# Order of the first feed-forward visits, and ten warm-up matmuls, in a float32 H3 + FFN kernel

## The chip, the cores and the metric

The kernel runs on one core of a Trainium2 chip. The metric is the device time of one execution in microseconds (us); lower is better. Its engines work side by side, each with its own instruction stream: TensorE (PE in the profile, its weight loads PEld), VectorE (DVE), ScalarE (ACT), GpSimd (POOL) and SyncE (SP), which here only issues DMAs.

## The reference

```
xn  = layernorm(q)                                   # q: 2048 x 576
kv  = shift_conv(k, 4 taps) * v
y   = irfft(rfft(kv, 4096) * rfft(ssm_k, 4096))[:2048] + kv * ssm_D
out = q + xn * y + relu(xn @ w1) @ w2                # w1: 576 x 4608, w2: 4608 x 576
```

Everything is float32. `q` has two uses: it is the input of the layer norm and it is added to the result.

## The kernel before

**Numbers.** A product of float32 matrices is made of three products of rounded parts: high by high, high by low, low by high. So each operand is split: ScalarE makes the high part by a copy into the rounded type, VectorE (activations) or GpSimd (weights, `split_lo`) makes the low part by a subtraction.

**Feed forward.** The 16 row tiles (128 rows each) form four row blocks of four tiles. The 4608 hidden columns form 18 chunks of 256 (`n`, two parts `j` of 128). The kernel goes twice over the 18 chunks, with two row blocks each time. The list `visits` says in which order a chunk meets a row block; `s` is the slot (0 or 1) that holds a block's operands. Before the change the list begins (chunk 0, slot 0), (chunk 0, slot 1), (chunk 1, slot 1), (chunk 1, slot 0), (chunk 2, slot 0). In a visit of the first half `mm1` makes the hidden values, for each part j 14 matmuls of 512 columns (line 548) into one of two PSUM banks, and `relu` leaves a high part `hh` (ScalarE, line 530) and a low part `ll` (VectorE, line 531). The second product is cut into units: `phase` queues eight units (four row tiles, two halves of 288 output columns) for one or two chunks, and `fill` issues them between the parts of later visits: as many as make up two chunks' worth at a time. A unit has 6 matmuls for each chunk (line 611), gathers in one of three PSUM buffers, and VectorE adds it to `acc` (line 615 for the first row block, 619 for others). The second half of the feed forward uses another form of the first product (`quad`, line 524), which the change does not touch.

**The start.** Input tiles of the first block are loaded in two pairs by SP and ACT. `keep_warm` runs matmuls on a zero tile (line 1082). `first_xT` takes the first block's rows: centred on VectorE or ScalarE, transposed by TensorE (line 255) and split into the operands `b1`, `b2`, `xr`; `WARM_TILE` gives how many warm-up matmuls the code puts behind the transposes of each of the four tiles. The division by the standard deviation is left to line 615. The second block (`second_xT`) is treated otherwise: statistics (line 172), `inv_std`, then `normalized` (line 187), transposes (line 271), splits. It is issued in one piece after the first visit and one `fill`.

**Weights.** `load_w1` loads a chunk of w1 into one tile `r1` (a single buffer with ten slots of 256 columns, five of which are used in the first half), `load_w2` half a chunk of w2 (two buffers). `split_plain`, `split_rest` and `split_w2` split them; the results lie in pools `g` and `w2` of four buffers each. `at_turn` puts a split's ScalarE part behind the latest relu that was issued.

**Order.** The code's order is a priority. A scheduler that simulates the program fixes each engine's instruction stream ahead of the run: it may put an instruction that it holds ready ahead of an earlier one that waits. `tc.issue_after` puts the instructions of a block behind a given one of the same engine. On the chip each stream runs in order.

**Convolution.** `conv` is a generator with three stages: forward transforms of the kernel and of kv (line 664), the middle (line 883), the inverse (lines 1024 and 1025). `tick` advances it in step with the feed forward, whose work counts in columns; `START` is the amount of feed forward ahead of its first step, and enters the rate as well:

```python
clock = {"ffn": 0.0, "conv": 0.0, "until": START, "done": False}
rate = FFT_TOTAL / (SHARE * FFN_TOTAL - PAUSES * PAUSE - START)
```

Of the kernel before, what the change touches and what calls it, by code (L numbers as in the profile page):

```python
# [10 lines left out]
F32 = mybir.dt.float32  # L11
F32R = mybir.dt.float32r
# [5 lines left out]
P = 128  # L18
# [8 lines left out]
FT = 2  # L27
FC = FT * P
NPAIR = DFF // FC
# [10 lines left out]
GR = P // (2 * A2)  # L40
NG = A1 // GR
N_WARM = 21
WARM_TILE = (0, 4, 0, 2)


W_PLAIN = 2 * 14 * 512
W_STAGE = (12 * HR, 12 * HR, 12 * HR + 2 * 512, 6 * HR + 2 * 512)
W_UNIT = 12 * NH
PAUSE = 16000
START = 12000  # L50
SHARE = 0.97


# [56 lines left out]
def h3_ffn_kernel(ctx: ExitStack, tc, x, k, v, shift_k, ssm_k, ssm_D, w1, w2, fwd, inv, mid, out):  # L110
# [35 lines left out]

    acc = {}

    def halves(u):

        return slice(u * A1, (u + 1) * A1), slice((1 - u) * A1, (2 - u) * A1)
# [8 lines left out]
    def load_x(t, tag, bufs, **queues):  # L160
        pair = xp.tile([P, 2, D], F32, tag=tag, name=f"acc{t}", bufs=bufs)
        move(pair, x, slice(t, t + 2), **queues)
        return pair

    def load_acc(t, **queues):
        pairs[t] = load_x(t, f"acc{t // BT % HB}", BT // 2, **queues)
        acc[t], acc[t + 1] = pairs[t][:, 0, :], pairs[t][:, 1, :]

    def stats(t, src):
# [40 lines left out]
    def split_low(c, ps, s):  # L210

        if c == 4:
            xr = ops[s, "xr"]
            done["act"] = nc.scalar.activation(xr[:64, :], ps[:64, :], AF.Copy)
            done["dve"] = nc.vector.tensor_tensor(xr[64:, :], ps[:64, :], xr[:64, :],
                                                  OP.subtract)
            return None
        to = ops[s, "b2" if c % 2 else "b1"][:, :, c // 2]
        last = nc.scalar.activation(to[:, 0], ps, AF.Copy)  # L219
        nc.vector.tensor_tensor(to[:, 1], ps, to[:, 0], OP.subtract)  # L220
        return last

    def row_tiles(s, name):
        t = scratch(s, name)
        return [t[:, i * D:(i + 1) * D] for i in range(BT)]

    def plain_tiles(s):
        for name in ("b1", "b2", "xr"):
            operand(s, name)

    def first_xT(srcs):

        plain_tiles(0)
        ps = []
        for c in range(5):
            ps.append(ps_o.tile([P, 512], F32, tag="o", name=f"psx{c}") if c >= 3 else fft_psum())
        neg = xp.tile([P, BT], F32, tag="neg", name="neg", bufs=1)
        behind = None
        rows = row_tiles(0, "xn0")
        for t in range(BT):  # L240
            xn = rows[t]
            if t % 2 == 0:
                with tc.issue_after(behind.ins) if behind else nullcontext():
                    stats(t, srcs[t])
                    behind = centred(xn, srcs[t], t)
            else:
                nc.scalar.activation(xn, srcs[t], AF.Copy, scale=-1.0 / D,
                                     accum_out=neg[:, t:t + 1])
                done["act"] = nc.scalar.activation(xn, srcs[t], AF.Identity,
                                                   bias=neg[:, t:t + 1])  # L250
                with tc.issue_after(done["act"].ins):
                    (split_plain if t == 1 else split_rest)(0, 0)
            for c in range(5):
                w = min(P, D - c * P)
                nc.tensor.transpose(ps[c][:w, t * P:(t + 1) * P], xn[:, c * P:c * P + w], ident)
            keep_warm(WARM_TILE[t])
        for c in range(5):
            last = split_low(c, ps[c], 0)
            if c == 1:
                with tc.issue_after(last.ins):  # L260
                    split_plain(0, 1)
        with tc.issue_after(done["dve"].ins):
            for t in range(1, BT, 2):
                stats(t, srcs[t])
            inv_std(0, BT)

    def turned(c, xn):
        w = min(P, D - c * P)
        ps = fft_psum()
        for i in range(BT):  # L270
            nc.tensor.transpose(ps[:w, i * P:(i + 1) * P], xn[i][:, c * P:c * P + w], ident)  # L271
        return ps
# [5 lines left out]

    def second_xT(srcs):

        plain_tiles(1)
        with tc.issue_after(done["acc"].ins):
            for t in range(BT + 2, HT):
                stats(t, srcs[t])
            inv_std(BT, BT)
        xn = row_tiles(1, "xn1")
        for cols in (slice(0, P), slice(P, D)):
            for i, row in enumerate(xn):
                normalized(row, srcs[BT + i], BT + i, cols)
        for c in range(5):  # L290
            split_low(c, turned(c, xn), 1)

    def later_xT(b):

# [128 lines left out]

    def load_w1(n):
        f0 = (n % NPAIR) * FC
        r1 = wp.tile([P, 10, FC], F32, tag="r1", name=f"r1_{n}", bufs=1)
        for o, step in ((0, P), (P, FC - P)) if n == 0 else ((0, FC),):
            f, to = slice(f0 + o, f0 + o + step), slice(o, o + step)
            queue = nc.gpsimd if n == 0 and o == 0 else nc.sync
            queue.dma_start(r1[:, :4, to], w1[:4 * P, f].rearrange("(c p) f -> p c f", p=P))  # L430
            for h in range(2):
                queue.dma_start(r1[64 * h:64 * h + 64, 4, to], w1[4 * P:, f])
        raw_w[n] = r1
        weights[n] = {}

    def load_w2(n, h):
        f0 = (n % NPAIR) * FC
        r2 = wp.tile([P, FT, NH], F32, tag="r2", name=f"r2_{n}_{h}", bufs=2)
        nc.sync.dma_start(r2, w2[f0:f0 + FC, h * NH:(h + 1) * NH]
                          .rearrange("(j p) d -> p j d", p=P))  # L440
        raw_w[n, h] = r2

    def group(n, k):
        return wp.tile([P, 2, 4, P], F32R, tag="g", name=f"g{n}_{k}", bufs=4)

    def split_into(n, hi, lo, src):
# [14 lines left out]
    def split_rest(n, j=None):  # L461
        f = slice(0, FC) if j is None else slice(j * P, (j + 1) * P)
        hi, lo = (m[:, f] for m in rest_flat(n))
        split_into(n, hi, lo, raw_w[n][:, 4, f])
# [41 lines left out]
    def split_w2(n, h):  # L506
        r2 = raw_w[n, h]
        t = wp.tile([P, 2, FT, NH], F32R, tag="w2", name=f"w2_{n}_{h}", bufs=4)
        with at_turn(n):
            nc.scalar.activation(t[:, 0], r2, AF.Copy)  # L510
        last = split_lo(t[:, 1], r2, t[:, 0])
        weights[n]["w2", h] = t
        return last
# [556 lines left out]
    for t in range(0, BT, 2):  # L1070
        load_acc(t, queues=(nc.sync, nc.scalar))
    load_w1(0)
    for h in range(2):
        load_w2(0, h)
    table = const.tile([P, 1], F32, name="table")
    nc.vector.memset(table, 1.0)
    nc.scalar.activation(table, table, AF.Sqrt)
# [10 lines left out]
    first_xT(acc)  # L1088
    with tc.issue_after(done["act"].ins):
        split_rest(0, 1)  # L1090
    for t in range(BT, HT, 2):
        load_acc(t)
    load_w1(1)
    for h in range(2):
        with tc.issue_after(done["act"].ins):
            done["pool"] = split_w2(0, h)
        load_w2(1, h)
    visits = []
    for half in range(HALVES):
        for m in range(NPAIR):  # L1100
            visits += [(half * NPAIR + m, (m + half + v_) % 2) for v_ in range(2)]
    ahead = (step for b_ in range(HB, NB) for step in later_xT(b_))

    def split_next(n, second, st):
# [21 lines left out]
        elif n + 1 < HALVES * NPAIR:  # L1126
# [4 lines left out]
            else:  # L1131
                sum_w(n + 1, st)

    for q, (n, s) in enumerate(visits):
        half, m = divmod(n, NPAIR)
        b = half * HB + s
        second = q % 2
        if q == 1:
            fill()
            second_xT(acc)  # L1140
        parts = quad(n, s, q % 2) if half else None
        for st in range(4):
            if half:
                next(parts)
            elif st % 2 == 0:
                mm1(n, s, st // 2)
                if q == 0:
                    done["acc"] = lows[-1]
            if q == 0 and st == 2:
                second_stats(acc)  # L1150
            split_next(n, second, st)
            if st == 1 and n:
                split_w2(n, second)
                if n + 1 < HALVES * NPAIR:
                    load_w2(n + 1, second)
            if half:
                tick(W_STAGE[st])
            if q > 3 and (st % 2 or st == 2 and q % 2):
                next(ahead, None)
            fill()  # L1160
        if m == NPAIR - 1 and not half:
            fetch(s, ("b1", "b2", "xr"))
        if n == NPAIR - 2 and not half:
            for _ in ahead:
                pass
            fetch(s, ("t",))
        last = m == NPAIR - 1
        if second == 0:
            phase([n] if m == 0 else [n - 1, n], s, b, last)
        elif last:  # L1170
            phase([n], s, b, True)
        if half == 1 and m == 0:
            base = HT + (1 - second) * BT
            for t in range(base, base + BT, 2):
                load_acc(t)
# [30 lines left out]
```

## Time and profile before

| | |
|---|---|
| runs | 1070.07 us median of 3 (1069.26 to 1071.27) |
| profiled execution, span from first to last instruction | 1071.0 us |
| TensorE busy | 1054.1 us (98%), 7147 matmuls |
| VectorE busy | 748.2 us (70%) |
| ScalarE busy | 549.7 us (51%) |
| GpSimd busy | 397.5 us (37%) |
| mean granted TensorE clock | 0.994 |
| DMA, mean | 191 GB/s |

The page of the profile has no other figure for the profiled execution's own time than its span. A line of a timeline reads: start, duration (for a merged group from its first start), engine, line of the code, operation, output <- input, shape, count, and in brackets the idle time of the engine just before and what ended it. A line of stretches reads: stretch, its length, busy time and count of each engine, granted clock, DMA share, GB/s.

### The profile page before, as it was taken

To read this page: it belongs to the slowest core of one execution; us is meant where nothing else is said; L and a number is where in the kernel's file an instruction comes from. 1 tells how busy PE (TensorE), PEld (TensorE's weight loads), DVE (VectorE), ACT (ScalarE), POOL (GpSimd) and SP (SyncE) were. 2 spreads that over 40 slices of the span, in tenths; PEclk is the share of its full clock that TensorE was granted. 3 is DMA by queue.
4 is the path that set the end of the run, shared out by engine and by line. 5 is a ranking of instruction groups with operands and counts; after the bars stand their busy time and mean duration, and the time that the engine had idled before them with its cause. 6 is when DMAs were issued, how large, how long until landed. Compare 5 with 4: busy or idle time off the path is not lost.

```text
span 1071.0 us, 19976 instructions
## 1 busy us (share of the span) xinstructions
PE 1054.1 (98%) x7147; PEld 991.6 (93%) x7147; DVE 748.2 (70%) x1314; ACT 549.7 (51%) x1201; POOL 397.5 (37%) x398
## 2 busy tenths in 40 slices
PE   7999999999999999999999999999999999999998
PEld 5789999899999999999999999999999998999998
DVE  5437777789876788752487887778777773666764
ACT  4225556534433434332387777777777763444430
POOL 3133333333333332223334434433434444454541
PEclk9999999999999999999999999999999999999999
DMA  7674757687857666755985556655645549866844
GB/s 183 142 176 127 201 163 204 177 244 225 237 165 179 185 179 200 238 153 185 306 247 180 162 168 185 180 181 170 196 141 177 170 147 295 256 220 193 246 144 111
DMA packets 156303, 204.45 MB, mean 191 GB/s; under 512 B 32845, under 2 KB 122703, under 8 KB 155180
## 3 DMA queue, kind: packets, MB, share of 16 engines
q1 hardware_dynamic: 143308, 189.00, 59.6%
q0 software_dynamic: 12576, 13.44, 5.5%
q8 instruction: 56, 0.92, 0.4%
q10 hardware_dynamic: 320, 0.74, 0.3%
q14 instruction: 43, 0.35, 0.1%
HBM read 133.92 MB, written 55.05 MB: 176 GB/s over the span
## 4 chain that ended last, share of the span: by engine, by line
PE 92%; DMA 3%; DVE 3%; ACT 1%; issue 1%; SPq 0%; ACTq 0%; DVEq 0%
PE pso L611 41%; PE psh L548 22%; PE psb L524 12%; PE psf L883 7%; PE psa L524 6%; PE psf L664 3%; DMA zo<-zy 1%; DMA acc<-in_x 1%; PE psf L1024 1%; PE psf L1025 1%; DMA both<-in_k 0%; DVE bn L172 0%; PE psf L271 0%; ACT k L914 0%; ACT k L913 0%
## 5 line engine op out<-in xcount | busy, mean ns | idle before, releaser
L611 PE MATMUL pso<-w,hh 128*128 128x288 f32 x2304 | 468.9, 295 | 1.2 <-DVE acc L615 0.8
L611 PEld LDWEIGHTS pso<-w,hh 128*128 128x128 f32 x2304 | 372.4, 188 | 9.4 <-ACT hh L530 1.3
L611 PE MATMUL pso<-w,ll 128*128 128x288 f32 x1152 | 328.4, 295 | 0.5 <-DVE both L719 0.5
L419 POOL TENSOR_TENSOR g<-r,g 128x256 fp32r<-128x256 f32 (+2 forms) x145 | 168.3, 1167 | 415.7 <-ACT g L448 386.1
L548 PE MATMUL psh<-b,g 128*128 128x512 f32 x864 | 219.8, 398 | 0.2 <-ACT b L219 0.2
L611 PEld LDWEIGHTS pso<-w,ll 128*128 128x128 f32 x1152 | 212.9, 188 | 1.6 <-DVE both L719 0.7
L548 PEld LDWEIGHTS psh<-b,g 128*128 128x128 f32 x864 | 158.5, 190 | 31.1 <-ACT b L219 0.5
L619 DVE TENSOR_TENSOR acc<-pso,acc 128x288 f32<-128x288 f32 x224 | 98.4, 450 | 73.2 <-PE pso L611 72.2
L419 POOL TENSOR_TENSOR w<-r,w 128x576 fp32r<-128x576 f32 x72 | 113.6, 1579 | 53.4 <-ACT w L510 53.2
L530 ACT ACTIVATE hh<-psh 128x512 fp32r<-128x512 f32 x72 | 43.0, 597 | 139.2 <-PE psh L548 139.1
L531 DVE SCALAR_TENSOR_TENSOR ll<-psh,hh 128x512 fp32r<-128x512 f32 x72 | 49.5, 688 | 71.2 <-ACT hh L530 70.9
L524 PE MATMUL psb<-t,g 128*128 128x256 f32 x648 | 96.0, 280 | 0.3 <-DVE psa L579 0.3
L448 ACT ACTIVATE g<-r 128x256 fp32r<-128x256 f32 (+2 forms) x145 | 76.7, 543 | 28.2 <-DMA r<-in_w 19.1
L524 PEld LDWEIGHTS psb<-t,g 128*128 128x128 f32 x648 | 85.9, 188 | 0.7 <-DVE psa L579 0.6
L477 POOL TENSOR_TENSOR r<-r 128x256 f32<-128x256 f32 x72 | 61.4, 872 | 39.7 <-DMA r<-in_w 38.4
L524 PE MATMUL psa<-b,g 128*128 128x256 f32 x432 | 63.2, 281 | 0.3 <-ACT psa L575 0.3
L524 PE MATMUL psb<-b,g 128*128 128x256 f32 x432 | 59.5, 284 | 0.0
L524 PEld LDWEIGHTS psa<-b,g 128*128 128x128 f32 x432 | 56.6, 188 | 0.6 <-ACT psa L575 0.6
L524 PEld LDWEIGHTS psb<-b,g 128*128 128x128 f32 x432 | 55.9, 192 | 0.2
L615 DVE SCALAR_TENSOR_TENSOR acc<-pso,rstd,acc 128x288 f32<-128x288 f32 x80 | 40.5, 510 | 15.3 <-PE pso L611 14.9
L926 DVE TENSOR_TENSOR k<-psf,k 128x288 f32<-128x288 f32 x64 | 29.0, 454 | 31.0 <-ACT sw L925 30.4
L530 ACT ACTIVATE hh<-psa 128x512 fp32r<-128x512 f32 x36 | 21.5, 598 | 55.5 <-PE psa L524 55.3
(134 smaller groups left out, 1684.1 us busy)
## 6 DMA issues: line engine op xcount, KB each, us to landing
r<-in_w SPq DMA_DIRECT2D x72, 288.0 KB, 3.9
zy<-vo SPq DMA_DIRECT2D x64, 288.0 KB, 2.9
zo<-zy SPq DMA_DIRECT2D x32, 576.0 KB, 5.1
r<-in_w SPq DMA_DIRECT2D x35, 512.0 KB, 4.7
zk<-zk SPq DMA_DIRECT2D x64, 144.0 KB, 2.6
ztk<-zk SPq DMA_DIRECT2D x32, 288.0 KB, 3.5
ztx<-zx SPq DMA_DIRECT2D x32, 288.0 KB, 3.5
k<-k SPq DMA_DIRECT2D x64, 144.0 KB, 3.3
```

The source lines that it names most:

```text
L419: return nc.gpsimd.tensor_tensor(dst, src, hi, OP.subtract)
L448: nc.scalar.activation(hi, src, AF.Copy)
L477: nc.gpsimd.tensor_tensor(dst, a, b, op)
L524: nc.tensor.matmul(ps, a, m, start=start and i == 0, stop=i == len(seq) - 1, skip_group_check=not start)
L530: done["act"] = nc.scalar.activation(hh, ps, AF.Relu)
L531: lows.append(nc.vector.scalar_tensor_tensor(ll, ps, 0.0, hh, op0=OP.max, op1=OP.subtract))
L548: nc.tensor.matmul(ps, a, m, start=i == 0, stop=i == len(seq) - 1)
L611: nc.tensor.matmul(ps[:, :NH], a, m, start=c == 0, stop=c == len(seq) - 1)
L615: done["acc"] = nc.vector.scalar_tensor_tensor(acc[t][:, dc], ps[:, :NH], rstd[:, t:t + 1], acc[t][:, dc], op0=OP.mult, op1=OP.add)
L619: done["acc"] = nc.vector.tensor_tensor(acc[t][:, dc], ps[:, :NH], acc[t][:, dc], OP.add)
L664: nc.tensor.matmul(ps[:, :NH], w[:, n, :], stk, start=n == 0, stop=n == 1)
L883: nc.tensor.matmul(ps[:, :NH], a, m[:, cols], start=n == 0, stop=n == 2)
```

## The change

1. The visits now begin (chunk 0, first block), (chunk 1, first block), (chunk 0, second block), (chunk 1, second block); from chunk 2 on the order is the old one. The two blocks of the first half change slots (`place`), so that the slots of the later visits fit.
2. The second product of chunks 0 and 1 is issued in pairs for both blocks; chunk 2 is single for the second block, as chunk 0 was for the first.
3. w1's chunk 1 is loaded right behind chunk 0, into the five unused slots of its tile, and split at once; two of its three split tiles lie in the first block's spent row buffer. w2's chunk 0 is loaded behind the second block's rows. The splits and loads of the first seven visits stand in a table, `opening`.
4. `second_xT` becomes a generator; it is issued ahead of the third visit, with a `fill` in each of three gaps.
5. `WARM_TILE` goes from (0, 4, 0, 2) to (0, 10, 0, 2), `START` from 12000 to 24000.

```diff
-WARM_TILE = (0, 4, 0, 2)
+WARM_TILE = (0, 10, 0, 2)
-START = 12000
+START = 24000
...
+    def place(b):
+
+        return 1 - b if b < HB else b - HB
...
     def second_xT(srcs):
 
-        plain_tiles(1)
+        s = place(1)
+        plain_tiles(s)
         with tc.issue_after(done["acc"].ins):
             for t in range(BT + 2, HT):
                 stats(t, srcs[t])
             inv_std(BT, BT)
-        xn = row_tiles(1, "xn1")
+        xn = row_tiles(s, "xn1")
...
-        for c in range(5):
-            split_low(c, turned(c, xn), 1)
+        yield
+        for cs in ((0, 1, 2), (3, 4)):
+            for c in cs:
+                split_low(c, turned(c, xn), s)
+            yield
...
     def load_w1(n):
         f0 = (n % NPAIR) * FC
-        r1 = wp.tile([P, 10, FC], F32, tag="r1", name=f"r1_{n}", bufs=1)
+        if n == 1:
+            r1 = raw_w[0, "more"]
+        else:
+            r1 = wp.tile([P, 10, FC], F32, tag="r1", name=f"r1_{n}", bufs=1)
+        if n == 0:
+            raw_w[0, "more"] = r1[:, 5:]
...
     def group(n, k):
+        if n == 1 and k:
+            if not extra:
+                extra["g"] = scratch(place(0), "g1")
+            at = (k - 1) * 8 * P
+            return (extra["g"][:, at:at + 8 * P].bitcast(F32R)
+                    .rearrange("p (m c f) -> p m c f", m=2, c=4))
         return wp.tile([P, 2, 4, P], F32R, tag="g", name=f"g{n}_{k}", bufs=4)
...
     load_w1(0)
-    for h in range(2):
-        load_w2(0, h)
...
+    load_w1(1)
     for t in range(BT, HT, 2):
         load_acc(t)
-    load_w1(1)
     for h in range(2):
-        with tc.issue_after(done["act"].ins):
-            done["pool"] = split_w2(0, h)
-        load_w2(1, h)
-    visits = []
+        load_w2(0, h)
+    for j in range(FT):
+        split_plain(1, j)
+    split_rest(1)
+    visits = [(0, place(0)), (1, place(0)), (0, place(1)), (1, place(1))]
     for half in range(HALVES):
-        for m in range(NPAIR):
+        for m in range(0 if half else 2, NPAIR):
             visits += [(half * NPAIR + m, (m + half + v_) % 2) for v_ in range(2)]
...
+    def later_w2(n, h):
+        with tc.issue_after(done["act"].ins):
+            split_w2(n, h)
+        if n + 1 < HALVES * NPAIR:
+            load_w2(n + 1, h)
+
+    opening = {(0, 1): [(later_w2, 0, 0)], (0, 3): [(later_w2, 0, 1)],
+               (1, 1): [(later_w2, 1, 0)], (1, 2): [(load_w1, 2)], (1, 3): [(later_w2, 1, 1)],
+               (3, 0): [(split_plain, 2, 0)], (3, 1): [(split_plain, 2, 1)],
+               (3, 3): [(split_rest, 2), (load_w1, 3)],
+               (5, 1): [(later_w2, 2, 0)], (6, 0): [(later_w2, 2, 1)]}
+    rest_of_block = second_xT(acc)
     for q, (n, s) in enumerate(visits):
...
-        b = half * HB + s
+        b = HB + s if half else 1 - s
         second = q % 2
-        if q == 1:
-            fill()
-            second_xT(acc)
+        if q == 2:
+            for _ in rest_of_block:
+                fill()
...
-                if q == 0:
+                if q < 2:
                     done["acc"] = lows[-1]
...
-            split_next(n, second, st)
-            if st == 1 and n:
-                split_w2(n, second)
-                if n + 1 < HALVES * NPAIR:
-                    load_w2(n + 1, second)
+            for what, *args in opening.get((q, st), ()):
+                what(*args)
+            if q > 3:
+                split_next(n, second, st)
+                if st == 1 and n > 2:
+                    later_w2(n, second)
...
-        if second == 0:
-            phase([n] if m == 0 else [n - 1, n], s, b, last)
+        if q in (1, 3):
+            phase([0, 1], s, b, False)
+        elif q > 3 and second == 0:
+            phase([n] if m == (0 if half else 2) else [n - 1, n], s, b, last)
```

More of the change, by code (lines that the diff above doesn't have):

```diff
@@ L165, in load_acc @@
     def load_acc(t, **queues):
-        pairs[t] = load_x(t, f"acc{t // BT % HB}", BT // 2, **queues)
+        pairs[t] = load_x(t, f"acc{place(t // BT)}", BT // 2, **queues)
         acc[t], acc[t + 1] = pairs[t][:, 0, :], pairs[t][:, 1, :]
@@ L231, in first_xT @@
     def first_xT(srcs):
-        plain_tiles(0)
+        plain_tiles(place(0))
         ps = []
@@ L238, in first_xT @@
         behind = None
-        rows = row_tiles(0, "xn0")
+        rows = row_tiles(place(0), "xn0")
         for t in range(BT):
@@ L257, in first_xT @@
         for c in range(5):
-            last = split_low(c, ps[c], 0)
+            last = split_low(c, ps[c], place(0))
             if c == 1:
@@ L441, in load_w2 @@
         raw_w[n, h] = r2
+    extra = {}
     def group(n, k):
+        if n == 1 and k:
[4 more added lines that the diff above has]
+                    .rearrange("p (m c f) -> p m c f", m=2, c=4))
         return wp.tile([P, 2, 4, P], F32R, tag="g", name=f"g{n}_{k}", bufs=4)
```

## The prediction

> **What bounds the kernel now.** I read the page first (engines, slices, chain), then a table of stretches for the first 53 us, then the timeline of those stretches, and last a table of 3.41 us pieces for the clock.
>
> ```profile
> span 1071.0 us, 19976 instructions
> PE 1054.1 (98%) x7147; PEld 991.6 (93%) x7147; DVE 748.2 (70%) x1314; ACT 549.7 (51%) x1201; POOL 397.5 (37%) x398
> PE 92%; DMA 3%; DVE 3%; ACT 1%; issue 1%; SPq 0%; ACTq 0%; DVEq 0%
> ...
> 8.31:14.20 5.89, 2.63 (x22) 2.10 (x21) 1.57 (x5) 3.03 (x7) 1.72 (x2) 0.99 1.11 270
> 14.20:22.86 8.66, 8.44 (x28) 6.19 (x28) 6.47 (x17) 4.57 (x11) 4.56 (x4) 0.81 0.79 215
> 22.86:32.88 10.02, 7.43 (x49) 6.50 (x49) 9.29 (x31) 1.16 (x3) 1.30 (x1) 1.00 0.64 147
> 32.88:44.61 11.73, 11.42 (x48) 8.70 (x48) 5.59 (x13) 3.50 (x7) 0.00 (x0) 0.85 0.70 148
> 44.61:53.00 8.39, 8.39 (x43) 7.16 (x44) 2.06 (x3) 2.95 (x6) 2.71 (x3) 1.00 0.27 80
> 250.00:500.00 250.00, 250.00 (x1501) 227.16 (x1500) 184.60 (x290) 99.53 (x198) 78.54 (x77) 1.00 0.68 195
> ```
>
> The rows of stretches give length, then busy time with count of PE, PEld, DVE, ACT, POOL, then granted clock, DMA share, GB/s. TensorE is the bound: 92% of the chain, and no idle at all between 250 and 500 us. So the time falls only by what TensorE loses, and the amount of matmul work does not change here except for six warm-up matmuls. The loss sits in the first 45 us. To size it I need the price of dense work, from the chain of waits, where a line is a run of matmuls back to back:
>
> ```profile
> 250.95 3.26 PE psh L548 x14
> 214.49 3.19 PE pso L611 x24
> ```
>
> That is 0.233 us for a matmul of the first product and 0.133 for one of the second. A transpose costs at most 2.63/22 = 0.12. Three stretches against their dense price:
> 14.20 to 22.86, the first block's chunk 0: 28 x 0.233 = 6.52, so 2.14 lost.
> 22.86 to 32.88, eight units of six matmuls: 48 x 0.133 = 6.38, so 3.64 lost.
> 32.88 to 44.61, twenty transposes and the second block's chunk 0: 2.40 + 6.52 = 8.92, so 2.81 lost.
> Together 8.6 us. From 44.61 on TensorE is busy in every microsecond.
>
> Part of that is the clock, in pieces of 3.41 us (same columns):
>
> ```profile
> 7.29:10.71 3.42, 2.34 (x16) 1.41 (x14) 0.84 (x3) 1.47 (x3) 0.11 (x1) 1.00 1.08 224
> 10.71:14.12 3.41, 1.31 (x10) 1.05 (x10) 1.55 (x4) 2.33 (x6) 1.61 (x2) 1.00 1.09 298
> 14.12:17.53 3.41, 3.33 (x7) 2.41 (x8) 3.12 (x5) 3.41 (x9) 1.84 (x3) 0.50 0.87 199
> 31.19:34.60 3.41, 2.03 (x11) 1.03 (x10) 3.30 (x14) 0.58 (x1) 0.00 (x0) 1.00 1.04 223
> 34.60:38.01 3.41, 3.41 (x14) 3.01 (x15) 2.00 (x5) 1.36 (x4) 0.00 (x0) 0.50 1.03 215
> 901.60:905.00 3.40, 1.17 (x9) 1.20 (x10) 1.27 (x4) 0.96 (x2) 3.25 (x5) 1.00 1.08 403
> 905.00:908.40 3.40, 3.40 (x17) 3.40 (x17) 0.32 (x1) 0.67 (x3) 0.06 (x1) 0.50 0.69 258
> ```
>
> Three times a piece with TensorE busy for 1.17 to 2.03 us is followed by a piece at clock 0.50; the piece with 2.34 us busy is not. The starts of the slow pieces (14.12, 34.60, 905.0) lie 6 and 261 steps of 3.41 us apart. Each costs 1.7 us. Two of the three lie in the 8.6 us; the other 5.2 us are waits: 0.44 in the first stretch, 3.64 in the second, 1.11 in the third.
>
> **The change, part by part.**
>
> Order of the work. Today after chunk 0 of the first block TensorE has only eight units of one chunk (6.4 us) to do while the second block's rows are made ready; it runs out:
>
> ```profile
> 21.54 1.10 PE L548 MATMUL psh<-xr,g 128*128 128x512 f32 x4
> 22.21 0.60 ACT L530 ACTIVATE hh<-psh 128x512 fp32r<-128x512 f32 x1 [1.70 <-PE psh L548]
> 22.84 0.69 DVE L531 SCALAR_TENSOR_TENSOR ll<-psh,hh 128x512 fp32r<-128x512 f32 x1 [1.52 <-ACT hh L530]
> 26.92 1.53 DVE L172 BATCH_NORM_STATS2 bn<-acc 128x6 f32<-128x288 f32 x4
> 32.48 2.81 DVE L187 TENSOR_SCALAR xn<-acc,mv,rstd 128x128 f32<-128x128 f32 x8
> 32.88 2.26 PE L271 MATMUL psf<-ident,xn 128*128 128x128 f32 x8 [1.29 <-DVE xn L187]
> ```
>
> After, chunk 1 of the first block (28 matmuls, 6.5 us) follows at once, and then eight units of twelve matmuls (8 x 12 x 0.133 = 12.8 us). The second block's chain on VectorE now begins behind chunk 1's last low part. Chunk 0 ends at 22.6 as today (clock drop kept, see below). Chunk 1 must write the same two banks: the first is read until 22.84 + 0.69 = 23.53, so TensorE stands for 0.9 us, a wait that units cover today. Chunk 1 ends at 30.0, its last low part about 1.5 later (0.60 + 0.69 and hand-over): 31.5. From the last statistics to the first normalized columns took 32.48 - 26.92 = 5.6 us and to the last one 8.4: first transposes near 37.5, rows done near 40, five splits of about 0.7 end near 43.4. TensorE's own work goes from 30.0 through 12.8 + 2.4 to 45.2. So the chain is covered by about 2 us, and the 3.64 us go. For waits inside the transposes I keep all of today's 1.11, the nearest row; the ends are 0 (all covered by units) and 3.6 (today's starving comes back whole). The second clock drop goes, because the piece with the transposes is now filled with units.
>
> Chunk 1's weights. The load (three DMAs on SP) moves from 17.34 to where the two loads of w2 chunk 0 stood, ahead of the second block's four x loads; w2 chunk 0 goes behind those. SP issues as many DMAs as before:
>
> ```profile
> 4.14 2.81 SPq L439 DMA_DIRECT2D r<-in_w  x2
> 17.34 0.39 SPq L430 DMA_DIRECT2D r<-in_w  x1
> 15.22 1.28 POOL L419 TENSOR_TENSOR g<-r,g 128x512 fp32r<-128x512 f32 x1 [1.96 <-ACT g L448]
> 16.66 1.26 ACT L510 ACTIVATE w<-r 128x576 fp32r<-128x576 f32 x2
> 17.42 2.82 POOL L419 TENSOR_TENSOR w<-r,w 128x576 fp32r<-128x576 f32 x2
> r<-in_w SPq DMA_DIRECT2D x72, 288.0 KB, 3.9
> ```
>
> 640 KB replace 576 KB ahead of the x loads, so those land at about the same time. ACT is free for the new splits at 16.7 (where it takes w2 now), POOL then does 1.28 + 1.28 + 0.7 and ends near 20.8, before 23.5: no cost. They go into the spent row buffer, whose transposes are over by 14.2: no wait. Chunk 2's weights (load after chunk 1's splits near 21, splits during the second block's chunk 1) have some 20 us: nothing.
>
> w2. Chunk 1's first half can be loaded only when POOL has split chunk 0's. That split stands behind the first relu on ACT: 22.8 + 0.63 + 1.41 + 3.9 + 0.63 + 1.41 = 30.8, about 31.2 with hand-overs. The units start at 30.0 and can do chunk 0's half of three units (three PSUM buffers, 18 x 0.133 = 2.4 us) without it, to 32.4. Hidden by 1.2 us; I take 0.2, from 0 to 3 if a load stands in front.
>
> Warm-up. The four and two matmuls that the code puts among the transposes do not run there:
>
> ```profile
> 1.21 7.30 PE L1082 MATMUL psw<-warm 128*128 128x512 bf16 x27 [1.21 <-DVE table L1076]
> 3.74 4.27 PEld L1082 LDWEIGHTS <-warm 128*128 128x128 bf16 x20 [0.28 <-issue]
> 8.35 0.52 PE L255 MATMUL psf<-ident,xn 128*128 128x128 f32 x3
> 12.63 0.55 PE L255 MATMUL psf<-ident,xn 128*128 128x128 f32 x3 [3.01 <-DVE xn L193]
> 14.20 7.50 PE L548 MATMUL psh<-b,g 128*128 128x512 f32 x24 [0.25 <-ACT b L219]
> ```
>
> All 27 (21 + 4 + 2) run before the first transpose. I take it that all 33 will: 6 x 4.27/20 = 1.28 us more, the first ten transposes end near 10.9 instead of 9.6, and the 3.01 us wait before the next ones hides it; without that cover it would cost 1.28. The piece 10.71 to 14.12 then has 1.31 + 0.2 = 1.5 us busy, under the 2.03 that did not suffice: the drop at 14.12 stays and I keep its 1.7. Were the ten to run in the gap (9.6 to 11.8), the piece would have 2.4, over the 2.34 that did.
>
> [...]
>
> Pacing. START 24000 lets the convolution's stream begin at the eighth tick, in chunk 1's second half, where 12000 gave the fifth, the first unit. Its rate grows by under 1%, so it ends at the same place of the feed forward: nothing on average. Its loads meet TensorE late in the kernel (the piece at 901.60 holds 2.3 us of waiting plus 1.7 of clock after it), and a shifted stream may lose or gain that: I allow 4 us down and 3 up.
>
> Sum on the profiled execution: loss today 8.6; after: 0.44 + 1.7 + 0.9 + 1.1 + 0.2 = 4.3. Gain 4.3, span 1071.0 - 4.3 = 1066.7. The profiled span stands 0.9 above the median of the runs (1070.07; they spread from 1069.26 to 1071.27), so I forecast 1065.8. About 0.2%, 2.1 us, is what a measurement can tell from no change.
>
> **The rivals.**
> *The first clock drop goes too.* The scheduler puts the added matmuls in the gap before 12.63, or the 3.41 us grid lies otherwise in another execution. For it: the gap is there; against: all 27 run ahead of it today. 1065.8 - 1.7 = 1064.1.
> *Late wait lost.* The shifted stream misses the wait at 901: 1065.8 - 4 = about 1062. Only the place of a load decides it.
> *The gain is given back.* The second block's chain on VectorE has only 2 us of cover, and each of eight accumulations lies in it:
>
> ```profile
> L615 DVE SCALAR_TENSOR_TENSOR acc<-pso,rstd,acc 128x288 f32<-128x288 f32 x80 | 40.5, 510 | 15.3 <-PE pso L611 14.9
> both<-in_ssm_k SPq DMA_DIRECT2D x12, 384.0 KB, 8.3
> ```
>
> Eight of 0.51 are 4.1 us; if all go ahead of the chain, it ends near 47.5 and TensorE waits 2.3, and the transposes with it are thin again, so the second clock drop stays: 1065.8 + 2.3 + 1.7 = 1069.8, no change. Against it: three or four accumulations already lie in today's 5.6 us.
> *Slower.* The second row: a load of the convolution's kernel lands after 8.3 us. If SP issues those loads ahead of w2 chunk 1, the units miss it by 8.3 - 1.2 = 7.1 us: 1072.9. It decides from a delay of about 7.6 us (1.2 of cover, 4.3 of gain, 2.1 to be seen). Against it: the stream starts later than the free buffer.
>
> **How the numbers follow.** Forecast 1065.8: 0.42, its own range 1063.5 to 1068. First drop gone, 1064.1: 0.25. Late wait lost, 1062: 0.08. Given back, 1069.8: 0.18. Slower, 1072.9: 0.07. The range 1062 to 1070.5 leaves out the slower case, half of the late-wait case and the edges of others, some 0.18. Faster by more than 0.2% (under 1067.9) are the first three less a tail of the first, 0.73; within 0.2% that tail and the given-back case, 0.20; slower 0.07.
>
> **What would show it.** Right: 56 matmuls of the first product between 14 and about 30 with one break near 1 us; idle between 22 and 45 us down from 3 us to about 1; no piece at clock 0.50 near 35; work beyond 60 us in the same order some 4 us earlier; 33 warm-up matmuls ahead of the first transpose. Wrong: an idle time named after w2, after the second block's xn or after chunk 1's weights between 20 and 45 us, transposes later than 40, or new waits after 850 us that eat the gain.

## The result, and the profile after

The changed kernel takes 1077.38 us (median of 5 runs, 1073.56 to 1079.17) against 1069.26 us of the kernel before in the same series (5 runs, 1068.80 to 1071.27): a ratio of 1.0062, with an interval of 1.0040 to 1.0084. It is slower by some 0.6%, where 1065.8 was forecast. The profiled execution took 1079.17 us, the longest of the five, with a span of 1077.4.

The first two rows of the page after:

```profile
span 1077.4 us, 20001 instructions
PE 1054.3 (98%) x7153; PEld 992.8 (92%) x7153; DVE 742.6 (69%) x1314; ACT 549.6 (51%) x1201; POOL 396.9 (37%) x398
```

TensorE is busy for the same time as before (1054.3 against 1054.1 us), so the 6.4 us of the span are idle time. Where they arise shows in a table of stretches (length, then busy time and count of PE, PEld, DVE, ACT, POOL, granted clock, DMA share, GB/s). Of the kernel after:

```profile
0.00:50.00 50.00, 45.94 (x251) 35.93 (x252) 25.95 (x71) 17.99 (x35) 15.12 (x20) 1.00 0.88 209
50.00:250.00 200.00, 198.53 (x1186) 179.67 (x1184) 148.74 (x262) 99.21 (x220) 68.43 (x77) 1.00 0.66 180
250.00:500.00 250.00, 246.33 (x1466) 223.49 (x1467) 175.96 (x284) 96.47 (x193) 75.32 (x75) 0.99 0.68 191
...
850.00:1077.40 227.40, 215.02 (x1610) 210.78 (x1608) 133.80 (x251) 87.71 (x200) 93.51 (x104) 0.98 0.62 192
```

Of the kernel before:

```profile
0.00:50.00 50.00, 42.42 (x201) 31.14 (x202) 26.12 (x70) 16.57 (x33) 12.25 (x18) 0.93 0.72 170
...
850.00:1071.00 221.00, 213.38 (x1615) 209.80 (x1613) 136.01 (x253) 88.70 (x202) 94.63 (x104) 0.99 0.65 199
```

In the first 50 us TensorE does 50 matmuls more than before (six of them warm-ups), idles 4.1 us where it idled 7.6, and its clock is 1.00 where it was 0.93. Between 250 and 500, where it had not idled at all, it now idles 3.7 us; behind 850 it idles 12.4 us against 7.6.

To follow one and the same work through two profiles I count the matmul work that is done, at the dense prices (0.233 us for a 512-column matmul of the first product, 0.133 for a 288-column one, 0.117 for a 256-column one, of which twelve take 1.40 us at 874.68 in the kernel before, 0.11 for a transpose, of which eight start from 9.67 to 10.55 in the kernel after; 1035.6 us in all with the prices not rounded, warm-ups left out), and compare the times at which a given amount is done. A row says by how many microseconds a profiled execution is ahead of that of the kernel before; minus is behind. That one execution of the kernel before has two pieces of 3.41 us at granted clock 0.50 in its start (at 14.12 and 34.60) and one at 905.0; such a piece is called a slow piece below, and some of a lead is that they are missing elsewhere:

```
work done (us)           25    225   250   262   510   520   895   960   980   1000  span
after                   +7.1  +7.7  +5.7  +0.8  +0.8  -0.1  -0.1  -2.4  -2.5  -6.1  -6.4
```

The start gains 7.1 us. Then 6.9 are lost between 225 and 262 us of work, 0.9 near 515, and 6.3 in the last stage. The start first, from the timeline of TensorE of the kernel after:

```profile
1.21 8.63 PE L1101 MATMUL psw<-warm 128*128 128x512 bf16 x33 [1.21 <-DVE table L1095]
9.67 0.49 PE L259 MATMUL psf<-ident,xn 128*128 128x128 f32 x3
...
11.94 0.55 PE L259 MATMUL psf<-ident,xn 128*128 128x128 f32 x3 [1.01 <-DVE xn L197]
...
21.56 0.66 PE L632 MATMUL pso<-w,hh 128*128 128x288 f32 x3 [0.79 <-ACT w L531]
...
29.70 0.63 PE L569 MATMUL psh<-xr,g 128*128 128x512 f32 x2
...
33.67 0.54 PE L632 MATMUL pso<-w,hh 128*128 128x288 f32 x2 [0.58 <-DVE acc L636]
...
39.51 0.27 PE L275 MATMUL psf<-ident,xn 128*128 128x128 f32 x1
...
45.38 0.60 PE L275 MATMUL psf<-ident,xn 128*64 128x128 f32 x4
```

All 33 warm-ups run ahead of the first transpose. Chunk 1 of the first block ends at 30.3. Between 22 and 45 us there is one idle time, 0.58 us. The second block's transposes come at 39.5 to 45.7, between units, and wait for nothing.

What TensorE waits for behind 100 us (engine, line, what for: us in total, times, longest), in the kernel after:

```profile
PE psf L1045 <- DMA zo<-zy: 6.3, 4, 2.4
PE psf L685 <- DMA xs<-both: 4.9, 2, 3.1
PE psf L1045 <- ACT psa L596: 1.1, 1, 1.1
PE psf L904 <- DVE k L947: 0.9, 1, 0.9
```

These are 13.2 us, two smaller ones make 13.7. The two largest of before, where all together are 4.3:

```profile
PE psf L1024 <- DMA zo<-zy: 2.7, 2, 2.3
PE psf L664 <- DVE ks L658: 0.8, 1, 0.8
```

The line L685 (L664 before) is the convolution's forward transform, here that of kv, L1045 (L1024 before) its inverse. Three of the waits are followed by a slow piece, at 277.01, 905.07 and 1021.12, each worth 1.7 us by estimate (half of 3.41 us, at clock 0.50).

How the wait at 275.61 comes about stands in the timeline of all engines of the kernel after:

```profile
266.96 0.63 ACT L469 ACTIVATE g<-r 128x512 fp32r<-128x512 f32 x1 [3.81 <-DMA r<-in_w]
267.50 0.67 ACT L531 ACTIVATE w<-r 128x576 fp32r<-128x576 f32 x1
...
268.07 0.67 ACT L832 ACTIVATE both<-both 128x576 fp32r<-128x576 f32 x1
268.64 0.67 ACT L835 ACTIVATE xs<-both 64x576 fp32r<-64x576 f32 x1
...
269.63 0.68 ACT L835 ACTIVATE xs<-both 64x576 fp32r<-64x576 f32 x1
...
270.35 0.76 DVE L836 TENSOR_TENSOR both<-both 128x576 fp32r<-128x576 f32 x1 [2.92 <-ACT xs L835]
...
271.21 1.14 SPq L839 DMA_DIRECT2D xs<-both  x2
...
275.61 0.50 PE L685 MATMUL psf<-xs,wx 128*128 128x288 f32 x2 [3.07 <-DMA xs<-both]
```

Nothing here is a long operation. ScalarE stands 3.81 us for a late load of w1; the split of kv stands behind that in its stream and begins at 268.07, though VectorE had its rows done at 264.74; VectorE waits 2.92 us for ScalarE, SP's DMA, issued at 271.21, for VectorE, which ends at 271.11, and TensorE, whose stream holds the transform at a fixed place, 3.07 us for the DMA. The same transform in the kernel before, with the issue of its load:

```profile
270.38 1.32 SPq L818 DMA_DIRECT2D xs<-both  x2
...
273.89 0.43 PE L664 MATMUL psf<-xs,wx 128*128 128x288 f32 x2
```

It did not wait, but it began 3.5 us after the issue, and between 215 and 300 us of that profile such loads took 2.6 to 4.1 us to land (median 3.3). So there was little room before the change, in a place where no wait showed it. In the kernel after TensorE is ready for the transform at 272.54, 1.3 us after the issue.

In the last stage the inverse transform reads 576 KB per step (`zo`), in four buffers, with the load three steps ahead. The use of a buffer sets off the load that replaces it: between 880 and 1030 us SP's issues of these loads waited 19 times for the inverse's matmuls, 42.6 us in all. Issues on SP, and the steps on TensorE that waited, from the timeline after:

```profile
984.52 11.88 SPq L991 DMA_DIRECT2D zo<-zy  x6
...
1012.75 3.29 SPq L991 DMA_DIRECT2D zo<-zy  x3
...
990.15 0.37 PE L1045 MATMUL psf<-zo,wi 128*128 128x288 f32 x1 [1.68 <-DMA zo<-zy]
...
1020.54 0.37 PE L1045 MATMUL psf<-zo,wi 128*128 128x288 f32 x1 [2.42 <-DMA zo<-zy]
```

From issue to first use 5.6 and 7.8 us passed; these two loads took 5.5 and 7.65 us to land, the median of all is 5.8 (quoted below at the fifth buffer). The steps come in clusters of three or four within a few microseconds, and three loads ahead do not span a cluster.

### The profile page after: what moved, and what is told of

It reads as the page before. It is cut to its first block, busy times and chain, and to the rows that moved or that the text cites. A ratio compares the mean times of both kernels' runs of the same rounds, so it can differ in the third digit from the quotient of the medians.

```text
span 1077.4 us, 20001 instructions
## 1 busy us (share of the span) xinstructions
PE 1054.3 (98%) x7153; PEld 992.8 (92%) x7153; DVE 742.6 (69%) x1314; ACT 549.6 (51%) x1201; POOL 396.9 (37%) x398
## 5 line engine op out<-in xcount | busy, mean ns | idle before, releaser
L640 DVE TENSOR_TENSOR acc<-pso,acc 128x288 f32<-128x288 f32 x232 | 102.3, 450 | 73.8 <-PE pso L632 72.8
L498 POOL TENSOR_TENSOR r<-r 128x256 f32<-128x256 f32 x72 | 58.0, 826 | 37.4 <-DMA r<-in_w 36.1
L672 POOL DMA_DIRECT2D wx<-in_fwd x32 | 17.7, 555 | 96.8 <-PE psf L685 85.6
L636 DVE SCALAR_TENSOR_TENSOR acc<-pso,rstd,acc 128x288 f32<-128x288 f32 x72 | 36.4, 510 | 20.1 <-PE pso L632 19.6
```

Source lines behind the costliest of these rows:

```text
L498: nc.gpsimd.tensor_tensor(dst, a, b, op)
L636: done["acc"] = nc.vector.scalar_tensor_tensor(acc[t][:, dc], ps[:, :NH], rstd[:, t:t + 1], acc[t][:, dc], op0=OP.mult, op1=OP.add)
L640: done["acc"] = nc.vector.tensor_tensor(acc[t][:, dc], ps[:, :NH], acc[t][:, dc], OP.add)
L672: nc.gpsimd.dma_start(w, src)
```

## The experiments

The theories, with the letters that some expectations use. *Place* (A): `START` 24000 moves the convolution's stream to places where its loads are late; narrowed after the first runs to "within the new order, the later place" (A2). *New deal* (B): any edit deals the fixed streams anew, and the late waits with them, without regard to where `START` puts the convolution; it allows almost any time, so that only a regular effect of the place can speak against it. *Order* (C): the new order of visits costs the time, whatever `START` is. *Late w1* (D): the load of w1 behind which ScalarE stands is the cause of the waits near 250 to 276. *Buffers* (E): the last stage loses its time because three loads ahead are too few. The six added warm-ups were a further rival. The ratios are each to the kernel before on the same chip.

**First series** (kernel before: median 1071.46, 35 runs). One constant at a time is taken back, or the constants alone are put in.

`e1_warm4`, the changed kernel with

```diff
-WARM_TILE = (0, 10, 0, 2)
+WARM_TILE = (0, 4, 0, 2)
```

> The changed kernel with WARM_TILE back at (0, 4, 0, 2); every engine's instruction stream is otherwise the same, instruction for instruction. If the six added matmuls cost time, it is 1.3 us faster than the changed kernel's 1077.4; if they keep the clock up at the first matmuls, it is up to 1.7 us slower (a piece at clock 0.50 near 14 us); if they lie in the wait ahead of the second pair of tiles and do nothing, the same within 1 us. Neither theory of the late waits lets them change.

Measured: 1076.43 us, ratio 1.0033 (1.0011 to 1.0055). Its profile is ahead by 7.1 at 225 us of work and behind by 0.9 at 262: the loss does not come from the warm-ups. It has no slow piece at 14 us, although only 27 warm-ups run.

`e2_start12k`, the changed kernel with

```diff
-START = 24000
+START = 12000
```

> The changed kernel with START back at 12000. Theory A, the pacing: the stream stands 2.4 to 3.2 us of feed-forward work later against the feed forward and meets its loads late; with 12000 the late waits of TensorE (13.7 us behind 100 us, and three clock drops) go back to the 4.3 us and one drop of before, while the gain at the start (7.8 us) stays: about 1062 to 1064. Theory B, a new deal: the fixed streams are dealt anew by any edit and the late waits with them, without regard to START: another set of waits, between 4 and 15 us, so 1063 to 1078 and not at the same places.

Measured: 1072.70, ratio 1.0006 (0.9991 to 1.0021). The slowdown against the kernel before is gone. But a return to 12000 does not give the whole start gain: 2.3 us are lost on kv's transform at 266.69, and the lead of 5.9 at 895 is gone at the end, with waits for zo again. The place theory in its first form, by which 12000 would give 1062 to 1064, fell.

`e3_start12k_warm4`, both constants as before, so the order alone:

> The changed order of visits alone: START 12000 and WARM_TILE (0, 4, 0, 2). Both theories: as the run with START 12000 alone, within 2 us, since the warm-up matmuls change no other instruction; theory A 1062 to 1064. If the order of visits itself costs the time (theory C), it stays near 1077.

Measured: 1071.97, ratio 1.0003 (0.9987 to 1.0018). With four warm-ups or ten the time is the same within the intervals, and the order theory, by which it would stay near 1077, does not fit. Against `e1_warm4`, which differs from it by `START` alone and ran in the same series, it is 4.5 us faster: so much does `START` 24000 cost in the new order. This execution does have a slow piece at 14.11, and its lead at 25 us of work is 5.5 against 6.7 of `e2_start12k`.

`e4_consts_only`, the kernel before with

```diff
-WARM_TILE = (0, 4, 0, 2)
+WARM_TILE = (0, 10, 0, 2)
-START = 12000
+START = 24000
```

> The kernel before with only the two constants changed (START 24000, ten warm-up matmuls). Theory A: the late waits of the changed kernel appear without its gain at the start: 1070 + 9 to 14, so 1079 to 1084. Theory B: another deal, 1066 to 1080. Theory C: as before, 1068 to 1071.

Measured: 1074.65, ratio 1.0032 (1.0015 to 1.0049). The constants alone make the old order slower too, but mostly elsewhere: 0.5 us at 250 to 262 us of work (6.9 in the changed kernel between 225 and 262), and 4.3 at 895 to 960 with waits for zo; a slow piece stands at 988.97. The place theory gave 1079 to 1084 here, so it missed; it was narrowed after this run to the new order.

**Second series** (kernel before: 1069.97, 35 runs). `e5_start18k`, the changed kernel with a place between:

```diff
-START = 24000
+START = 18000
```

> The changed kernel with START 18000, which puts the first transform of kv at the same place of the feed forward as in the kernel before (after 200.1 us of its matmul work; 203.3 with 24000, 196.9 with 12000). Theory A2, the stream's place decides: the waits of 250 to 276 us go, since the kernel before has none there, and the lead of about 7 us at 225 us of work is still there at 300: some 1064 to 1066. Theory B, a new deal: the place has no such effect; a lead between -1 and 5 us at 300, 1066 to 1077.

Measured: 1068.19, ratio 0.9990 (0.9973 to 1.0006). The lead is 6.5 at 300 us of work and 9.0 at 895: the new order does not cost its gain, and the order theory falls. The time is above the 1064 to 1066 that the place theory gave, because the rest goes in the last stage, 5.0 us of waits for zo. With 18000 the first transform of kv stands in TensorE's stream behind 200.1 us of feed-forward work, as in the kernel before; with 24000 it stands behind 203.3, with 12000 behind 196.9.

`e6_w1_early` asks whether the late w1 is the cause. One permanent tile, whose halves alternate, so that a chunk's load is issued nearly one chunk earlier (seven of its eight stages):

```diff
+        if "all" not in raw_w:
+            raw_w["all"] = wp.tile([P, 10, FC], F32, tag="r1", name="r1", bufs=1)
+        r1 = raw_w["all"]
+        if n < NPAIR:
+            r1 = r1[:, 5 * (n % 2):5 * (n % 2) + 5]
...
+                if st == 0 and n + 2 < NPAIR:
+                    load_w1(n + 2)
```

> The changed kernel; in the first half w1's chunks take turns in the two halves of the same tile, so that a chunk's load is issued one chunk earlier (three stages of work more ahead of its split). Theory D, the late w1 load: ScalarE's stream waits for the load (5.4 us at 238, 3.8 at 267), the split of kv stands behind it and TensorE's first transform of kv waits for that; the waits at 250.6 and 275.6 us (4.9 us and a clock drop) go, ScalarE's waits for r in the first half fall from 23 us to under 8, lead at 300 us of work near 6 instead of 0.8, time 1071 to 1073. If the kv rows themselves are late (rival), those two waits stay.

Measured: 1074.80, ratio 1.0037 (1.0018 to 1.0056). ScalarE no longer waits for w1 anywhere between 200 and 285 us, where it had done so for 16.9 us. One of the two waits of TensorE is gone, the other stays; the waits of TensorE in that window, of this kernel:

```profile
PE psf L684 <- DMA xs<-both: 2.4, 1, 2.4
```

Half of the theory holds, and the time is above the 1071 to 1073 that it gave: of the 6.9 us between 225 and 262 us of work 4.1 are still lost. By this timeline other queues (VectorE and SP, and a wait of ScalarE for the transform's own scratch) are now late in place of the load of w1; that was not tested further.

`e7_zo5`, the changed kernel with a fifth buffer for `zo` and the load four steps ahead (the room comes from a smaller `low` tile):

```diff
-                    z = fp.tile([P, 2, D], F32R, tag="zt", name=f"zo{n}", bufs=4)
+                    z = fp.tile([P, 2, D], F32R, tag="zt", name=f"zo{n}", bufs=5)
...
-            for n in range(3):
+            for n in range(4):
...
-                        load_z(n + 3)
+                        load_z(n + 4)
```

> The changed kernel with a fifth buffer for the inverse transform's input, loaded four units ahead instead of three (the low part's buffers are cut to pay for it). Streams up to the last stage are those of the changed kernel. Theory E, loads against clusters of units: the four waits for zo (904.8, 933, 990, 1020; 6.3 us and two clock drops) shrink to under 2 us, time 1070 to 1073. If the loads are late for another reason (SP standing behind other waits), they stay and the time is 1076 to 1078. No effect ahead of 880 us in either.

Measured: 1068.56, ratio 0.9990 (0.9973 to 1.0006). What ended TensorE's idle time ahead of the inverse steps, and how long the loads took, first in the kernel after:

```profile
  DMA zo<-zy: 6.3, 4
...
DMA to landing us min/median/max: 3.8/5.8/9.3
```

and with the fifth buffer:

```profile
  ACT m L595: 1.4, 2
...
DMA to landing us min/median/max: 3.7/6.2/9.8
```

The loads take no less time, but nobody waits for them. From 262 us of work to the end the kernel after loses 7.2 us to the kernel before, this one gains 4.1. The waits for kv (2.18 and 2.82 us) are there as before.

`e8_both` puts the last two together:

> The changed kernel with both the earlier w1 loads and the fifth zo buffer. Theories D and E: the lead of about 7 us at the start is kept to the end: 1063 to 1066, faster than the kernel before. Theory B alone: one more deal, 1066 to 1078.

Measured: 1070.34, ratio 0.9999 (0.9979 to 1.0018). The two theories together gave 1063 to 1066, so this missed. It is not faster than the fifth buffer alone, although its profile leads by 5.3 at 262. It loses 1.5 near 515 (a wait for `k`) and 3.1 between 960 and the end; a wait for kv of 2.16 remains.

**Third series** (kernel before: 1070.57, 29 runs). `e9_before_zo5` is the kernel before with the edit of `e7_zo5`:

> The kernel before with the fifth zo buffer and nothing else. Theory E: its two waits for zo (903.8 and 1019.7, 2.7 us) and the clock drop at 905 go: 1065.5 to 1067 against 1070. It is also the fair rival of the next run: with the last stage's waits taken from both, what is left between them is the new order. If the fifth buffer only re-deals the last stage, 1068 to 1072.

Measured: 1066.52, ratio 0.9963 (0.9943 to 0.9983). The late waits of the kernel before were the same kind: of 2.7 us 0.6 is left.

`e10_start18k_zo5` is the changed kernel with `START` 18000 and the fifth buffer:

> The changed kernel with START 18000 and the fifth zo buffer. Theories A2 and E: the start's 7 us reach the end and the waits for zo of the last stage (897, 926, 1010; 5.0 us) go: 1062 to 1064, 3 to 4 us faster than the kernel before with five buffers. Theory B alone: a new deal of the last stage, 1065 to 1070.

Measured: 1062.02 (6 runs, 1060.69 to 1063.38), ratio 0.9918 (0.9893 to 0.9942), the fastest of all. Its span and its table of stretches:

```profile
span 1060.4 us, 20025 instructions
...
250.00:500.00 250.00, 249.47 (x1495) 226.56 (x1494) 176.28 (x279) 96.84 (x194) 80.05 (x78) 1.00 0.66 191
...
850.00:1060.40 210.40, 203.67 (x1554) 200.39 (x1552) 127.74 (x238) 82.71 (x189) 93.04 (x103) 1.00 0.66 204
```

and the three longest waits of TensorE behind 100 us:

```profile
PE psf L1044 <- ACT w L531: 1.3, 1, 1.3
PE psf L685 <- DMA xs<-both: 0.5, 1, 0.5
PE psf L1044 <- DMA zo<-zy: 0.5, 1, 0.5
```

With the late waits taken from both, the new order is worth 1066.52 - 1062.02 = 4.5 us.

`e11_start21500` and `e12_start28k` test the narrowed place theory with two more values, with nothing else changed:

```diff
-START = 24000
+START = 21500     (e11_start21500)
+START = 28000     (e12_start28k)
```

> The changed kernel with START 21500; kv's first transform stands at 200.1 us of feed-forward work, as with 18000 and in the kernel before, though the streams are another deal. A2, the place decides: the lead at 300 us of work is over 5 us, no wait for xs over 1 us. B, the deal decides: anything from -1 to 7. The last stage is a new deal in either; 1065 to 1072.

> The changed kernel with START 28000; kv's first transform stands at 203.3, as with 24000. A2: waits for xs near 250 to 276 us as with 24000, lead at 300 us of work under 3; time 1073 to 1079. B: anything; the lead at 300 between -1 and 7.

Measured: 1068.41, ratio 0.9977 (0.9955 to 1.0000), and 1074.66, ratio 1.0035 (1.0015 to 1.0056). The lead of each profiled execution, with the feed-forward work that stands ahead of kv's first transform in TensorE's stream:

```
START   work ahead   lead at 225   at 262   at 895   at the end   median of runs
12000   196.9            +7.3       +4.4     +5.9       0.0         1072.70
18000   200.1            +7.4       +6.5     +9.0      +5.5         1068.19
21500   200.1            +7.3       +6.2     +7.4      +3.5         1068.41
24000   203.3            +7.7       +0.8     -0.1      -6.4         1077.38
28000   203.3            +7.5       +0.1     -0.2      -2.7         1074.66
```

Within the new order the loss at kv's transform goes with the place: 200.1 keeps the lead but for about 1 us, 203.3 loses nearly all of it, both times, and 196.9 loses 3 us. The profiles of `e1_warm4` and `e7_zo5`, also at 203.3, lose it too (-0.9 and -0.1 at 262), and that of `e10_start18k_zo5`, at 200.1, keeps 6.9. Theory B gives no reason for that. ScalarE's waits go with it. For w1 between 200 and 285 us, in the kernel after and then in `e10_start18k_zo5`, whose place is 200.1:

```profile
ACT g L469 <- DMA r<-in_w: 16.9, 3, 7.7
```

```profile
ACT g L469 <- DMA r<-in_w: 6.9, 1, 6.9
```

At 203.3 one late load is followed by two more of over 3 us each. At 200.1 ScalarE waits long once, near 215; `e5_start18k` and `e11_start21500` have two more waits there, of 0.2 to 0.7 us. Why the old order at the same place (`e4_consts_only`) loses only 0.5 us there stays open. Its waits for w1 in that window are 1.38 and 2.12 us instead of 7.65, 5.43 and 3.81, but what makes the loads later in the new order was not tried. The table also shows the last stage: between 895 and the end every value of `START` loses, from 2.5 to 6.3 us, at steps that differ from one value to the next. There theory B is not refuted.

## Why the prediction was wrong

**What bounds the kernel.** Right: TensorE's busy time did not move, and the result is the sum of its idle time and its clock.

**The order of the work.** The mechanism was right. The gain came out larger, 7.1 us for the 4.3 forecast, but not all of it is shown to come from the order. Chunk 1 ends at 30.3 (30.0 forecast), the transposes begin at 39.5 (37.5 forecast). The 0.9 for the bank and 0.2 for w2 came as one wait of 0.79, named after the split of w2, and one of 0.58 for a PSUM buffer of the units. The 1.1 us inside the transposes did not come: units stand between them. The idle time of the first 50 us fell by 3.5 us (2.6 were forecast), and both slow pieces went, 3.4 us by the estimate, where one was forecast to stay. The first slow piece's absence is no merit of the ten warm-ups that could be shown: the kernel with four had no slow piece at 14 in `e1_warm4` and `e9_before_zo5`, and had one in the kernel before and in `e3_start12k_warm4`; with ten there was none in ten kernels. The second, near 34 us, came in the kernel before and in `e4_consts_only`, and in no kernel of the new order; but the old order of `e9_before_zo5` has neither piece, and its start leads that of the kernel before by 3.1 us. Also, the second pair of rows was ready 0.7 us sooner than before (its transposes begin at 11.94 instead of 12.63); in `e9_before_zo5` they begin at 12.04. So the start is worth between 3.9 us (the lead of `e10_start18k_zo5` over `e9_before_zo5` at 25 us of work, neither with a slow piece) and 7.1.

**The warm-ups' cost.** Right as far as shown: they end at 9.84 instead of 8.51, and the wait ahead of the later transposes shrinks from 3.01 to 1.01 us. But 27 of them end at 9.36 in `e1_warm4`, so two executions do not measure the six. The piece from 10.77 has 1.97 us of TensorE where 1.5 were forecast, and no slow piece follows.

**Pacing.** This is the step that failed: "Its rate grows by under 1%, so it ends at the same place of the feed forward: nothing on average." The end is indeed nearly the same (the last inverse step stands behind 874.9 us of feed-forward work, 877.7 before). But all that lies between moves: kv's first transform stands 3.2 us of feed-forward work later. I had weighed the mean of the stream's place, and allowed 4 us down and 3 up for one late wait that might move. What counts is each step's margin to its loads at its own place: in the stretch from 250 to 500 us, where the profile of before has no idle time, I took the absence of waits for the absence of a limit. The term is 13.5 us (from 7.1 ahead to 6.4 behind): 6.9 at kv's transforms (a wait of 1.83 at 250.60, then 3.07 at 275.61 and the 1.7 of clock behind it), 0.9 in the middle, 6.3 in the last stage, less 0.6 gained ahead of them.

The two constants are only part of it. `START` alone cost 4.5 us (`e1_warm4` against `e3_start12k_warm4`). With `START` left at 12000 the new order gains nothing either (ratio 1.0003): it puts kv's first transform at 196.9 instead of 200.1, and the lead is lost there and in the last stage as well. So the error was to put nothing for what the shifted stream meets, by whichever part of the change it is shifted. What made the loads of w1 late in the new order stays open.

With `START` 18000, and with the fifth buffer in both kernels, the new order is worth 4.5 us, and 4.3 were forecast. That they lie so close is in part luck: 1.7 of the 4.3 was a slow piece, and neither of the two profiles has one in its start.

**The rivals.** "The first clock drop goes too" happened, though all 33 warm-ups ran ahead of the gap; "late wait lost" did not: the wait at 901 is still there, 1.95 us at 904.76, and three more for zo stand beside it. "Given back" did not happen: the second block's rows came 2 us later than forecast and the units covered them. "Slower" gave the right side by another mechanism; the loads of the convolution's kernel did not get ahead of w2. Among the signs that were to show the prediction wrong were "new waits after 850 us that eat the gain": those came, and those near 250 to 276 were not on the list.

**The carrying over to the runs.** I compared a span with the median of the runs, 0.9 us below it. The profiled execution after took 1.8 us more than its span, so the two are not the same measure. The forecast does not suffer from it: it comes to the median less the gain, 1070.07 - 4.3.

## What to carry to other kernels

A constant that only shifts one stream against another changes no work, and so costs "nothing on average" only if every step of the stream has room; look for the margin of each (issue to landing against issue to use), above all where the profile shows no wait at all, for the list of waits shows no margin there. A shift can be tried at several values before it is judged: here five values of one constant spread over 9 us. When a local gain disappears, follow the lead over the old kernel by work done, not by time: it names the places where it is lost, and each can be tested by itself. A prefetch has to span the cluster in which its buffers are used, not the mean distance between uses: here one more buffer was worth 4 us in the old kernel and, with `START` 18000, let the new order keep its gain.

## What the runs showed of the hardware

The slow pieces of one execution start whole steps of 3.413 us apart: 184 steps from 277.01 to 905.07 and another 34 to 1021.12 in the kernel after, 6 from 14.12 to 34.60 and another 255 to 905.0 in the kernel before. The grid's place differs between executions: the slow pieces that start at 252.38 in `e7_zo5` and at 275.27 in `e1_warm4` lie 7.2 and 0.5 steps ahead of the one at 277.01. In the slow piece at 905.07 twelve matmuls of 256 columns start 0.213 us apart, where the dense price is 0.117; a piece full of them costs 1.5 us, so the 1.7 of the estimate is a little high. What follows the pieces that are only partly busy, in the kernel after:

```profile
10.77:14.18 3.41, 1.97 (x13) 1.23 (x11) 1.75 (x5) 2.58 (x7) 0.79 (x2) 1.00 1.09 300
14.18:17.59 3.41, 3.36 (x14) 2.75 (x15) 3.14 (x6) 3.25 (x8) 2.66 (x3) 1.00 1.00 228
...
273.60:277.01 3.41, 1.41 (x9) 1.39 (x10) 2.27 (x5) 1.55 (x3) 0.00 (x0) 1.00 1.09 288
277.01:280.42 3.41, 3.41 (x10) 2.75 (x10) 2.34 (x4) 0.46 (x1) 0.19 (x1) 0.50 1.02 265
...
986.99:990.40 3.41, 1.73 (x13) 1.44 (x12) 1.87 (x5) 1.00 (x2) 1.47 (x2) 1.00 1.02 387
990.40:993.81 3.41, 3.41 (x28) 3.32 (x28) 1.15 (x2) 1.00 (x2) 0.00 (x0) 1.00 0.98 366
```

in `e3_start12k_warm4`:

```profile
10.70:14.11 3.41, 1.69 (x11) 1.23 (x11) 1.75 (x5) 2.58 (x7) 1.53 (x2) 1.00 1.11 293
14.11:17.52 3.41, 3.18 (x8) 2.48 (x8) 3.14 (x6) 3.41 (x9) 2.37 (x3) 0.50 1.01 230
```

and in `e7_zo5`:

```profile
276.27:279.68 3.41, 1.59 (x10) 1.53 (x11) 1.96 (x5) 1.59 (x3) 0.00 (x0) 1.00 1.06 295
279.68:283.09 3.41, 3.41 (x19) 2.87 (x18) 2.92 (x5) 1.37 (x3) 0.54 (x1) 1.00 1.03 297
```

A wait of 3.07 us was followed by a slow piece in the kernel after, and one of 2.82 us at the same step was not in `e7_zo5`, where the piece ahead holds 1.59 us of work instead of 1.41. But TensorE's busy time of a piece does not decide alone: 1.69 us was followed by clock 0.50, as was 2.03 in the kernel before, while 1.59, 1.73 and 1.97 were not. The prediction's bound of 2.03 to 2.34 was therefore not a bound, and what decides is open.
